# Third copies of VectorE's groups by an accumulating transfer onto a buffer filled with the constant, in a fused attention and GEGLU block

## The chip, the cores and the metric

The kernel runs on one core of one Trainium2 chip. The metric is the device time of one execution in microseconds; lower is better. Two runs of the kernel before gave 807.44 and 808.38 us, median 807.91.

## The reference

One transformer block over 2048 tokens of width 512, in bf16, with a modulation computed from a vector `c`:

```python
mod = (silu(c) @ w_mod).reshape(1, 6, 1, -1)          # sa, ca, ga, sb, cb, gb
h = layernorm(x) * (1 + ca) + sa
q, k, v = heads(h @ wqkv)                             # 32 heads of 16
p = softmax(q @ k.T * 16 ** -0.5)
x = x + ga * ((p @ v) @ wo)
h = layernorm(x) * (1 + cb) + sb
x = x + gb * ((gelu(h @ w_gate) * (h @ w_up)) @ w_down)   # 1792 wide
```

The heavy part off TensorE is the softmax: 32 heads x 2048 x 2048 exponentials.

## The kernel before

**A planner writes the order.** The program has no loops on the chip. Python code (class `_Recorder`, `rec` at L219) records each instruction with its reads and writes, works out the semaphore waits, and keeps a model of when each engine is free and when each transfer lands (`model`, L297; `ISSUE`, L52, and `MARGIN`, L55, are the allowances of each kind of transfer in ns). `stream` (L1441) chooses what comes next by that model: it asks with `probe` (L327) when a step's inputs will be there, and issues it if that is soon enough. What it writes is a fixed list for each engine, and on the chip each engine works through its list in order, waiting for semaphores. If something lands later than the model said, everything behind it on the waiting engine is late too.

**The units.** Attention is cut into 64 units: a set of query columns by a group of four heads that lie on the four row strips of TensorE. A unit is 512 (four of them, the first two interleaved), 256 (52) or 128 (8) query columns wide, and is worked in rounds: 16, 8 or 4 of them, by width. A round is one 128 x 512 bank of scores for each of the four heads, so 2048 banks in all. TensorE computes the scores into two sets of three PSUM banks (`ps_sc`), ScalarE takes the exponentials of a set in one instruction (1536 wide, or 1024 where one bank goes to VectorE) into a ring of 15 slots, `E`, and TensorE multiplies them with the values into `ps_pv` (`pv_mms`, L1792). The units' products are taken in order: a unit starts when the one before has ended.

**VectorE's groups.** ScalarE is relieved by VectorE, which takes whole rounds: four banks, one for each head, called a group (or quad). VectorE converts a bank of scores to 16-bit integers that, read as bf16, are a stepwise approximation of the exponential (`bits`, L1712, a multiply and add, 128 x 512, PSUM to SBUF, into one of the buffers `kq`). Then come three copies of the whole group, 128 x 2048, each with a constant added (`SHIFT` is 32, 64, 96), into the buffers `sq` (`shift_task`, L1804). The converted group and its three copies are multiplied with four scaled versions of the values (`vaug` and `vs`), and the sum evens out the steps. So a group costs VectorE four conversions and three copies, and TensorE four times the products of a round. There are nine `sq` slots by name; which of them may be used depends on the stage (`room`, L1511): the first four always after "modB" (the modulation of the second half, done early in the kernel), others while the memory they overlap is free. A copy's slot is given back when its product has been issued (L1609).

`plain[u]` counts the rounds of unit u whose products are still to be taken from `E`; a group taken from the unit lowers it by one.

**Everything else is side work** that fills TensorE's and VectorE's gaps: the projections, the output projection, the feed-forward network set by set, with its weights streamed through SyncE's queue (SP) in 256 KB pieces, and the denominators of the softmax, which travel through small transfers on the same queue (`unit_end`, L1826). `background` (L1348) issues such steps on SP and VectorE when the model says they are due. The Pool engine works only in the first microseconds and once more for a mask.

**The planner's rules.** Fourteen numbers say how eager the planner is: how much slack ScalarE must have before side work is issued, how many candidates for groups it looks ahead, and so on. They come from `TUNE` (L63), a row for each stage of 64 banks, 33 rows for 32 stages; `RULES` (L62) is a common row that three of the stages use unchanged.

**The fillers.** `short` (L1427) adds up the columns of matmul work (weighted by the share of the array that they use) that the planner has issued in the last 3413 ns, and compares the sum with `FILL`, 3700. Where there is less, and TensorE has time, the planner adds matmuls whose result nobody uses: the identity times a tile of `x` (L1661, L1757), or a product with zeros (L1762). A thin stretch also lets side work go ahead of its credit (L1743).

Of the kernel before, what the change touches and what calls it, by code (L numbers as in the profile page):

```python
# [6 lines left out]
ALU = mybir.AluOpType  # L7
# [4 lines left out]
U16 = mybir.dt.uint16  # L12
# [10 lines left out]
NKT = S_TOK // P  # L23
VW = DH + 1
EPS = 1e-5
FILL = 3700
HALF = 0
GELU_C = 0.044715
TANH_C0 = float(np.sqrt(2.0 / np.pi))
# [19 lines left out]
NS = 3  # L49
NSQ = 4  # L50
FLOW = sum(a + n <= 1536 for a, n in SETS)
ISSUE = {"dd": 462, "de": 630, "db": 610, "dc": 400, "st": 410, "sd": 530, "se": 530, "ws": 450, "wu": 420, "wg": 510, "wd": 480, "ou": 400, "qo": 620}  # L52
SAFE = 0
EARLY = (800, 1000, 800)
MARGIN = {"db": 1200, "dd": 1800, "de": 1500, "qo": 1500, "st": 2300, "dc": 1500, "ws": 1500, "sd": 2000, "se": 1700, "wd": 1700, "wu": 1500, "wg": 1500}  # L55
FIRST = (2, 1, 2, 3)
STOP = ('ln2',)
STOPAT = 0
# [1 line left out]
ROUND = 200  # L60
STEP = 64
RULES = (600, 3500, 6, 120, 700, 150, 2, 9, 96, 30, 2, 1536, 100, 150)  # L62
TUNE = (  # L63
# [33 lines left out]
)  # L97
END = (0, None)
WAIT = 250
SLIP = 100  # L100


# [26 lines left out]
class _Recorder:  # L129
# [292 lines left out]
    def dma(self, eng, out, in_, sem, noncontig=False, late=0):  # L422
# [8 lines left out]
        run = min(int(a.ap[-1][1]) * mybir.dt.size(a.dtype) for a in (out, in_))  # L431
        return self.rec(eng, fn, [in_], [out], dma=sem, cost=(n, run, MARGIN.get(sem[:2], 0) + late))

    def emit(self, final):
        for s in self.count:
            self.sem[s] = self.nc.alloc_semaphore(s)
        val = {}
        for s, ops in self.bystream.items():
            n = 0
            for op in ops:  # L440
                if s in COMPUTE:
                    n += 1 if op.inc else 0
                else:
                    n += 16
                val[(s, op.seq)] = n
        prog = {e: [] for e in ALLENG}
        for op in self.ops:
            waits = tuple((s, val[(s, n)]) for s, n in op.waits.items())

            def run(e, op=op, waits=waits):  # L450
                for s, v in waits:
                    e.wait_ge(self.sem[s], v)
                ins = op.fn(e)
                if op.stream not in COMPUTE:
                    ins.then_inc(self.sem[op.stream], 16)
                elif op.inc:
                    ins.then_inc(self.sem[op.stream], 1)
            prog[op.eng].append(run)
        for s in final:
            prog["sp"].append(lambda e, s=s: e.wait_ge(self.sem[s], 16 * self.count[s]))  # L460
        with self.nc.Block() as block:
            for eng, starter in (("sp", block.sync), ("act", block.scalar), ("pe", block.tensor),
                                 ("dve", block.vector), ("pool", block.gpsimd)):
                def body(e, fns=prog[eng]):
                    for f in fns:
                        f(e)
                starter(body)


class _Kernel(_Recorder):  # L470
# [12 lines left out]
    def alloc(self):  # L483
# [71 lines left out]
        self.pv = ps("ps_pv", [P, 512], FP32)  # L555
        self.mi = ps("ps_mi", [P, 512], FP32)
        self.scr2 = self.dram("scr_rec", [4, 2048], FP32)
        self.wdg = self.dram("wd_scaled", [F, D], BF16).rearrange("(f p) n -> p f n", p=P)


    def prologue(self):
# [15 lines left out]
        for k in range(3):  # L577
            self.dma(sp, wq4[:, :, k, P:D], wqv[:, :, k, P:D], "wr%d" % k)
        self.dma(sp, self.wmod[:, :, 1024:3072], wmv[:, :, 1024:3072], "wm2")

        half = self.half
        self.memset(dve, self.warm, 0.0)
# [729 lines left out]
    def step(self, eng, t):  # L1312

        hold = None
        for tk in sorted(self.tasks, key=self.urgency):
# [3 lines left out]
            if "last" in self.have and eng == "dve" and t is not None:  # L1319
# [3 lines left out]
                if self.urgency(tk) == -3:  # L1323
                    hold = x if hold is None else min(x, hold)
                    if x > max(t, self.free[eng] + WAIT):
                        continue
                elif x > t or (hold is not None and max(x, self.free[eng]) + self.probed > hold + SLIP):
                    continue
            elif t is not None and self.probe(f) > t:
                continue  # L1330
# [15 lines left out]
        return n  # L1346

    def background(self, t):  # L1348
        while self.step("sp", max(self.free["sp"], t) + 40):
            pass  # L1350
        while self.free["dve"] <= t + self.tune[13] and self.step("dve", max(self.free["dve"], t) + 40):
            pass

    def force(self):
        if not self.step("sp", None) and not self.step("dve", None):
            assert self.step("act", None)

    def plan(self, ends, nsplit, begin):
# [82 lines left out]
    def stream(self):  # L1441
# [59 lines left out]
        wait = []  # L1501
        self.quad_free = list(range(NK + 1))
        self.sq_free = list(range(len(self.sq)))
        self.holds = {}
        self.users = [0] * (NKT // 4)
        soon = units[:4] + [u for u in units[4:] if u[0] == (0,)]
# [88 lines left out]
        def pv_do(x):  # L1595
# [10 lines left out]
            else:  # L1606
                q["ready"].remove((i, src))
                q["n"] -= 1
                if i:  # L1609
                    self.sq_free.append(q["slots"].pop(i))  # L1610
                if q["n"] == 0:
                    wait.remove(q)
# [179 lines left out]
    def pv_mms(self, rnd, acc, src, i, first, last):  # L1792
# [3 lines left out]
        for kk in range(kpb):  # L1796
            kt = r * kpb + kk
            v = self.vs[:, i - 1, kt % 4, VW * 8 * (self.part_of(kt // 4, dc) - dc):] if i else self.vaug[:, kt, :]
            for j in range(4):
                h = 8 * dc + 2 * j + ee  # L1800
                self.mm(acc[32 * j:32 * j + VW, 0:W], v[:, VW * h:VW * h + VW], src[j][:, W * kk:W * kk + W],
                        start=first and kk == 0, stop=last and kk == kpb - 1, tp=(0, 32 * j))

    def shift_task(self, q, i):  # L1804

        def f():
            s = self.room(self.sq_free, q["rnd"][0])[0]
# [300 lines left out]
```

## Time and profile before

| | |
|---|---|
| median of two runs | 807.91 us |
| profiled execution, its own time | 808.1 us |
| span of its instructions | 806.4 us |
| conversions of scores on VectorE, in the three largest groups | 412 |
| transfers on SP's queue | 57.99 MB in 97216 packets |
| work of Pool | 4.9 us, 13 instructions |

Reading it: PE is TensorE's matmuls, PEld its weight loads, DVE is VectorE, ACT ScalarE, POOL GpSimd, SP SyncE. A row of instructions names line, engine and operation, the tile written and those read with their shapes, and the count; then busy microseconds in all and the mean nanoseconds of one; then the idle time of the engine ahead of them and what ended it. In a table by stretch each engine's busy time is given with the number of its instructions, then the clock that TensorE was granted (1.00 is full speed), the busy share of the 16 transfer engines, and GB/s. Most instructions go through a helper and carry its line, so a tile's name tells more than the line. The rows that matter are shown in the prediction.

### The profile page before, as it was taken

Reading aid. Unit: us, or ns where it says so; the run is one execution under the profiler, and the core shown is the slowest. Engines: PE = TensorE matmul, PEld = TensorE weight load, DVE = VectorE, ACT = ScalarE, POOL = GpSimd, SP = SyncE. Lnnn points to the kernel's source line nnn. Section 1 sums busy time; section 2 is a strip of 40 time slices with the busy share of each in tenths; the row PEclk is TensorE's granted clock in tenths of the full one; section 3 lists DMA queues with packets and bytes.
Section 4 is the critical chain, followed back from the end, with each engine's and each line's share of the span. In section 5 each row is a group of like instructions: output and inputs, shape, how many; then the busy total and the mean of one; then the engine's idle time right before and its main releaser. Section 6 shows DMA issues by size and latency. Waiting matters only on the chain.

```text
span 806.4 us, 37404 instructions
## 1 busy us (share of the span) xinstructions
PE 749.7 (93%) x17203; PEld 373.9 (46%) x17203; DVE 748.8 (93%) x1514; ACT 778.1 (96%) x729; POOL 4.9 (1%) x13
## 2 busy tenths in 40 slices
PE   8899999998999989998999999989998999999998
PEld 4334344343543455344544554445443554456566
DVE  7878999999999999989999999999999999999874
ACT  6999999999999999999999999999999999999982
POOL 2000000000000000000000000000000000000000
PEclk9999999999999999999999999999999999999999
DMA  9100012240550055003430542034233532200000
GB/s 302 59 12 12 25 36 63 62 118 13 151 148 21 18 144 154 25 15 114 122 93 16 140 121 55 22 107 125 71 78 91 160 100 79 81 11 12 24 6 15
DMA packets 97904, 60.92 MB, mean 76 GB/s; under 512 B 16913, under 2 KB 95378, under 8 KB 97746
## 3 DMA queue, kind: packets, MB, share of 16 engines
q1 hardware_dynamic: 97216, 57.99, 25.4%
q8 instruction: 135, 2.21, 1.2%
q10 hardware_dynamic: 530, 0.53, 0.2%
q14 instruction: 23, 0.19, 0.1%
HBM read 51.74 MB, written 4.18 MB: 69 GB/s over the span
## 4 chain that ended last, share of the span: by engine, by line
ACT 79%; PE 13%; DVE 6%; DMA 1%; issue 1%; SPq 0%; DVEq 0%
ACT E L377 76%; PE ps_sc L364 5%; PE ps_mi L364 5%; PE ps_pv L364 3%; ACT wreg L377 2%; DVE mreg L389 1%; DVE dreg L389 1%; DVE wreg L394 1%; DVE wreg L398 1%; DMA xs<-in_A_x_dram 0%; DMA mreg<-in_B_w_up_dram 0%; DVE wreg L381 0%; DVE kq L389 0%; DVE hreg L381 0%; DVE hreg L389 0%
## 5 line engine op out<-in xcount | busy, mean ns | idle before, releaser
L377 ACT ACTIVATE E<-ps_sc 128x1024 bf16<-128x1024 f32 (+2 forms) x683 | 752.0, 1309 | 14.2 <-PE ps_sc L364 13.7
L364 PE MATMUL ps_sc<-qo,kT 32*128 32x256 bf16 (+2 forms) x2048 | 195.8, 273 | 18.3 <-ACT E L377 14.9
L364 PE MATMUL ps_sc<-qT,kT 32*128 32x256 bf16 (+3 forms) x2048 | 196.3, 273 | 16.7 <-ACT E L377 13.2
L364 PE MATMUL ps_pv<-E,vaug 128*17 128x256 bf16 (+2 forms) x3188 | 154.4, 273 | 1.3 <-DVE vaug L398 0.5
L389 DVE TENSOR_SCALAR dreg<-ps_sc 128x512 uint16<-128x512 f32 x200 | 135.4, 683 | 5.4 <-PE ps_sc L364 4.3
L364 PE MATMUL ps_mi<-wreg,mreg 128*32 128x256 bf16 x2816 | 109.4, 275 | 6.1 <-DVE wreg L398 3.7
L364 PEld LDWEIGHTS ps_sc<-qo,kT 32*128 32x128 bf16 x2048 | 60.6, 92 | 108.7 <-ACT E L377 90.6
L364 PEld LDWEIGHTS ps_sc<-qT,kT 32*128 32x128 bf16 (+1 forms) x2048 | 60.9, 92 | 103.7 <-ACT E L377 79.6
L364 PEld LDWEIGHTS ps_pv<-E,vaug 128*17 128x17 bf16 x3188 | 61.3, 89 | 57.8 <-issue 36.5
L389 DVE TENSOR_SCALAR kq<-ps_sc 128x512 uint16<-128x512 f32 x112 | 75.7, 684 | 10.0 <-PE ps_sc L364 9.4
L364 PEld LDWEIGHTS ps_mi<-wreg,mreg 128*32 128x32 bf16 x2816 | 64.2, 96 | 39.2 <-issue 20.9
L389 DVE TENSOR_SCALAR mreg<-ps_sc 128x512 uint16<-128x512 f32 x100 | 67.1, 682 | 1.7 <-PE ps_sc L364 1.5
L364 PE MATMUL ps_pv<-mreg,vs 128*17 128x256 bf16 (+2 forms) x1504 | 67.0, 270 | 1.3 <-DVE mreg L389 1.2
L389 DVE TENSOR_SCALAR mreg<-dreg 128x2048 uint16<-128x2048 uint16 x90 | 60.1, 679 | 1.4 <-PE ps_pv L364 1.3
L364 PEld LDWEIGHTS ps_pv<-mreg,vs 128*17 128x17 bf16 x1504 | 33.0, 91 | 14.5 <-issue 5.7
L364 PE MATMUL ps_mi<-hreg,wreg 128*32 128x512 bf16 (+1 forms) x496 | 37.4, 377 | 0.4 <-DVE qT L389 0.3
L394 DVE SCALAR_TENSOR_TENSOR wreg<-wreg,ps_mi 128x512 bf16<-128x512 bf16 x49 | 33.2, 678 | 1.2 <-ACT wreg L377 0.9
L381 DVE TENSOR_TENSOR wreg<-wreg 128x1024 bf16<-128x1024 bf16 (+1 forms) x56 | 34.2, 611 | 0.1
L398 DVE CAST wreg<-ps_mi 128x512 bf16<-128x512 f32 x49 | 33.4, 682 | 0.7 <-PE ps_mi L364 0.3
L389 DVE TENSOR_SCALAR mreg<-mreg 128x2048 uint16<-128x2048 uint16 x49 | 33.0, 680 | 0.0
L377 ACT ACTIVATE wreg<-wreg 128x1024 bf16<-128x1024 bf16 (+1 forms) x28 | 29.7, 1062 | 0.0
L389 DVE TENSOR_SCALAR mreg<-kq 128x2048 uint16<-128x2048 uint16 x40 | 27.0, 682 | 0.3 <-PE ps_pv L364 0.2
(201 smaller groups left out, 782.9 us busy)
## 6 DMA issues: line engine op xcount, KB each, us to landing
mreg<-in_B_w_up_dram SPq DMA_DIRECT2D x46, 256.0 KB, 3.1
mreg<-in_B_w_gate_dram SPq DMA_DIRECT2D x42, 256.0 KB, 3.2
dreg<-wd_scaled SPq DMA_DIRECT2D x18, 256.0 KB, 3.8
rb<-scr_rec SPq DMA_DIRECT2D x116, 32.0 KB, 2.3
mreg<-wd_scaled SPq DMA_DIRECT2D x12, 256.0 KB, 4.5
ereg<-wd_scaled SPq DMA_DIRECT2D x12, 256.0 KB, 4.0
mreg<-in_w_mod_dram SPq DMA_DIRECT2D x1, 2048.0 KB, 12.8
out_dram<-xs SPq DMA_DIRECT2D x15, 128.0 KB, 1.7
```

What stands on the lines that cost most here:

```text
L364: return self.rec("pe", lambda e: e.matmul(out, lhsT, rhs, start=start, stop=stop, tile_position=tp), [lhsT, rhs], [out], cost=(n, int(rhs ...
L377: return self.rec("act", lambda e: e.activation(out, in_, func, scale=scale, **kw), rd, wr, cost=self.cost("act", out, [in_], "act"))
L381: return self.rec(eng, lambda e: e.tensor_tensor(out, a, b, op), [a, b], [out], cost=self.cost(eng, out, [a, b], "tt"))
L389: return self.rec(eng, lambda e: e.tensor_scalar(out, a, s1, s2, **kw), rd, [out], cost=self.cost(eng, out, [a], "ts") + 60 * (len(rd) - 1 ...
L394: return self.rec("dve", lambda e: e.scalar_tensor_tensor(out, a, s, b, op0=op0, op1=op1), rd, [out], cost=self.cost("dve", out, [a, b], " ...
L398: return self.rec(eng, lambda e: e.tensor_copy(out, in_), [in_], [out], cost=self.cost(eng, out, [in_], "ts"))
```

## The change

- For a group's third copy, where conditions hold, VectorE does nothing. A buffer of `sq` has been filled ahead with the constant 96 in every 16-bit element, by a transfer from a DRAM tensor of 128 x 2048 such elements (`prefill`, on SP, 512 KB); and a transfer issued from Pool adds the converted group onto it (`dma_add`, 512 KB, with `accum_op`). The product of that copy then waits for this transfer.
- The conditions: a filled buffer exists; and the unit still has at least `DISTANT` (13) times its width / 512 rounds in `plain`. Buffers are filled one at a time, after "modB" and before the last scores, while more than one slot is free and one of the first four is among them.
- The planner gets allowances for the two transfers: "px" (the fill) 500 ns of issue and 1000 ns of margin, "ax" (the addition) 1400 and 2500, and it counts the addition as three times its bytes (`ADDED`).
- In the prologue Pool writes the constant into one buffer, ahead of its other work, and SP stores it to DRAM behind the loads.
- `background` and `force` also step tasks on Pool.
- The rows of `TUNE` are replaced by 32 times `RULES`.
- `FILL` becomes 1 at the top of the file, and the same name is set again further down, where it is also the number of buffers filled ahead. `short` reads the same name, so its threshold is 1 column.

The diff, without the 33 rows that go:

```diff
-FILL = 3700
+FILL = 1
...
-ISSUE = {"dd": 462, "de": 630, "db": 610, "dc": 400, "st": 410, "sd": 530, "se": 530, "ws": 450, "wu": 420, "wg": 510, "wd": 480, "ou": 400, "qo": 620}
+ISSUE = {"dd": 462, "de": 630, "db": 610, "dc": 400, "st": 410, "sd": 530, "se": 530, "ws": 450, "wu": 420, "wg": 510, "wd": 480, "ou": 400, "qo": 620, "px": 500, "ax": 1400}
...
-MARGIN = {"db": 1200, "dd": 1800, "de": 1500, "qo": 1500, "st": 2300, "dc": 1500, "ws": 1500, "sd": 2000, "se": 1700, "wd": 1700, "wu": 1500, "wg": 1500}
+MARGIN = {"db": 1200, "dd": 1800, "de": 1500, "qo": 1500, "st": 2300, "dc": 1500, "ws": 1500, "sd": 2000, "se": 1700, "wd": 1700, "wu": 1500, "wg": 1500, "px": 1000, "ax": 2500}
...
-TUNE = (
...
-)
+TUNE = (RULES,) * 32
 END = (0, None)
 WAIT = 250
+DISTANT = 13
+ADDED = 3
+FILL = 1
+KEEP = 1
...
+    def dma_add(self, out, in_, sem):
+        n = mybir.dt.size(out.dtype)
+        for _, k in out.ap:
+            n *= int(k)
+        return self.rec("pool", lambda e: e.dma_start(out, in_, accum_op=ALU.add), [in_, out], [out], dma=sem, cost=(ADDED * n, 4096, MARGIN["ax"]))
...
+        self.scx = self.dram("shift_row", [P, 2048], U16)
...
+        self.memset(pool, self.sq[NSQ - 1].bitcast(U16), SHIFT[NS - 1])
+        self.dma(sp, self.scx, self.sq[NSQ - 1].bitcast(U16), "px_")
...
-                elif x > t or (hold is not None and max(x, self.free[eng]) + self.probed > hold + SLIP):
+                elif x > t or (hold is not None and max(x, self.free[eng]) + (self.probed if isinstance(self.probed, float) else 0) > hold + SLIP):
...
     def background(self, t):
+        if "modB" in self.have and "last" not in self.have and len(self.filled) < FILL and len(self.sq_free) > KEEP and min(self.sq_free) < NSQ:
+            self.prefill()
+        while self.step("pool", max(self.free["pool"], t) + 40):
+            pass
...
-        if not self.step("sp", None) and not self.step("dve", None):
+        if not self.step("sp", None) and not self.step("pool", None) and not self.step("dve", None):
...
+        self.filled = []
...
-                if i:
+                if i in q["slots"]:
                     self.sq_free.append(q["slots"].pop(i))
...
+    def prefill(self):
+        s = self.sq_free.pop(self.sq_free.index(next(x for x in self.sq_free if x < NSQ)))
+
+        def f():
+            self.dma("sp", self.sq[s].bitcast(U16), self.scx, "px%d" % s)
+        self.task([("sp", f)], ("px", s))
+        self.filled.append(s)
+
     def shift_task(self, q, i):
+
+        if i == NS - 1 and self.filled and self.plain[q["rnd"][0]] * 512 >= DISTANT * q["rnd"][0][3]:
+            s = self.filled.pop(0)
+
+            def g():
+                self.dma_add(self.sq[s].bitcast(U16), self.kq[q["k"]].bitcast(U16), "ax%d" % s)
+                if self.probing is None:
+                    q["slots"][i + 1] = s
+                    q["ready"].append((i + 1, [self.sq[s][:, 512 * x:512 * x + 512] for x in range(4)]))
+            self.task([("pool", g)], ("add", q["rnd"][0]), lambda: ("px", s) in self.have)
+            return
```

33 rows, old and new, of the table TUNE are left out of this document.

## The prediction

> **What bounds the kernel now.** I read the page first (busy shares, then the chain that ended last), then the busy time by stretch, then the groups of ScalarE and VectorE by form.
>
> ```profile
> span 806.4 us, 37404 instructions
> ...
> PE 749.7 (93%) x17203; PEld 373.9 (46%) x17203; DVE 748.8 (93%) x1514; ACT 778.1 (96%) x729; POOL 4.9 (1%) x13
> ...
> ACT 79%; PE 13%; DVE 6%; DMA 1%; issue 1%; SPq 0%; DVEq 0%
> ```
>
> ```profile
> 20.00:780.00 760.00, 710.48 (x16676) 346.88 (x16673) 721.91 (x1428) 757.43 (x698) 0.56 (x1) 1.00 0.26 72
> 340.00:360.00 20.00, 18.86 (x389) 8.10 (x386) 18.01 (x35) 19.39 (x19) 0.00 (x0) 0.91 0.06 16
> ```
>
> The columns of the second fence are the stretch, then busy us of PE, weight loads, DVE, ACT and POOL, granted clock, DMA share and GB/s. Between 20 and 780 us ScalarE idles 2.6 of 760 us and VectorE 38: the exponentials on ScalarE set the end, and VectorE, which takes what rounds it can off ScalarE, is nearly as full. So freed VectorE time is worth something only through more rounds moved over to it. POOL does nothing, and the DMA share is 0.26: both have room.
>
> ```profile
> L377 ACT ACTIVATE E<-ps_sc 128x1536 bf16<-128x1536 f32 x282 | 416.2, 1562 | 2.7 <-PE ps_sc L364 2.4
> L377 ACT ACTIVATE E<-ps_sc 128x1024 bf16<-128x1024 f32 x393 | 398.0, 1143 | 1.1 <-PE ps_sc L364 0.9
> ```
>
> ```profile
> L389 DVE TENSOR_SCALAR dreg<-ps_sc 128x512 uint16<-128x512 f32 x200 | 135.4, 683 | 5.4 <-PE ps_sc L364 4.3
> L389 DVE TENSOR_SCALAR kq<-ps_sc 128x512 uint16<-128x512 f32 x112 | 75.7, 684 | 10.0 <-PE ps_sc L364 9.4
> L389 DVE TENSOR_SCALAR mreg<-ps_sc 128x512 uint16<-128x512 f32 x100 | 67.1, 682 | 1.7 <-PE ps_sc L364 1.5
> L389 DVE TENSOR_SCALAR mreg<-dreg 128x2048 uint16<-128x2048 uint16 x90 | 60.1, 679 | 1.4 <-PE ps_pv L364 1.3
> ```
>
> ```profile
> 219.29 1.89 DVE L389 TENSOR_SCALAR mreg<-dreg 128x2048 uint16<-128x2048 uint16 x3
> 221.20 0.69 DVE L398 CAST wreg<-ps_mi 128x512 bf16<-128x512 f32 x1
> ```
>
> The first three VectorE rows are conversions, 412 of them, so 103 groups of four. A copy lasts 679 ns, but three in a row take 1.89 us and the next instruction starts 1.91 us after the first: instructions overlap, and a copy, or a conversion, costs 0.6 to 0.64 us of the queue. I take 0.60. A group costs VectorE 4 conversions and 3 copies, 4.2 us. It saves ScalarE four times the difference between an activation of 1536 and one of 1024, 4 x (1562 - 1143) ns = 1.68 us.
>
> **The change, part by part.**
>
> (1) Copies off VectorE. A 256-wide unit has 8 rounds. Its first group leaves a count of 7, and 7 x 512 is over 13 x 256; its second leaves 6, which is too few. So at most one group a unit is served: the 52 units of that width, less those at whose turn no filled buffer waits or a round has been consumed, and less those before "modB", plus two or three 512-wide ones. I take 45 copies, bounds 25 and 52. VectorE saves 45 x 0.60 = 27 us. Both engines are full and must end together, so with x more groups ScalarE shortens by 1.68x and VectorE's load by 27 - 4.2x; equal at x = 27 / 5.88 = 4.6 groups, and the kernel by 1.68 x 4.6 = 7.7 us. With 25 copies it is 4.3, with 52 it is 8.9. A filled buffer takes one of four copy buffers while it waits; cover is the three others and those that some stages add. A group's own buffer is held until its addition's matmuls, some 9 us instead of 2; groups come 680 us / 100 = 6.8 us apart, so two are held at a time, of four. If that cover is gone, groups are refused and the term shrinks: the last rival.
>
> (2) The fillers. The name FILL now stands twice and is 1, also for the rule that adds matmuls when TensorE's work of the last 3.4 us is under 3700 columns. They vanish. The stretches below lie on the grid of 3413 ns on which the clock changed.
>
> ```profile
> 86.23:89.64 3.41, 2.75 (x53) 1.36 (x50) 3.38 (x9) 3.41 (x4) 0.00 (x0) 1.00 0.00 0
> 192.04:195.45 3.41, 2.36 (x44) 0.73 (x36) 2.11 (x10) 3.41 (x4) 0.00 (x0) 1.00 0.05 7
> 618.66:622.07 3.41, 2.53 (x46) 1.00 (x46) 2.39 (x11) 3.41 (x3) 0.00 (x0) 1.00 0.28 68
> 352.45:355.86 3.41, 2.27 (x48) 0.84 (x46) 3.35 (x6) 3.41 (x4) 0.00 (x0) 1.00 0.00 0
> 355.86:359.27 3.41, 3.41 (x56) 1.44 (x59) 3.15 (x7) 2.82 (x3) 0.00 (x0) 0.50 0.04 7
> ```
>
> The same stretches, fillers alone (the columns are now PE, weight loads, DVE, POOL, clock, DMA):
>
> ```profile
> 192.04:195.45 3.41, 1.01 (x12) 0.35 (x12) 0.00 (x0) 0.00 (x0) 1.00 0.05 7
> 618.66:622.07 3.41, 0.93 (x12) 0.44 (x12) 0.00 (x0) 0.00 (x0) 1.00 0.28 68
> ```
>
> After the emptiest stretch (2.27 us busy) the next ran at half clock; TensorE lost 1.7 us of 3.41, and ScalarE idled 3.41 - 2.82 = 0.59 us. Without their 1.01 and 0.93 us of fillers two other stretches would be at 1.35 and 1.60 us, below it. With similar places early in the kernel I take seven such stretches: 7 x 0.59 = 4 us. Bounds: 0, if new work lies there, and 7 x 1.7 = 12 us. The Trainium skill ("TensorE: Matmul & The Clock Gate", "Why this matters for your kernels") says that one idle window of about 3 us takes the clock down; by that rule gaps as short as these cost nothing and this term would be 0. The trace differs: 2.27 busy us of 3.41 were followed by half clock, and I go by the row.
>
> (3) Fills and additions. A fill moves 512 KB by SP, an addition 512 KB by POOL.
>
> ```profile
> mreg<-in_w_mod_dram SPq DMA_DIRECT2D x1, 2048.0 KB, 12.8
> ...
> mreg<-in_w_mod_dram ACTq DMA_DIRECT2D x1, 512.0 KB, 4.8
> ```
>
> A fill should land in about 4.8 us; it is issued as soon as the one before is used, so about a unit's time (680 us over 50 units, 13.6 us) ahead of its own use: nothing there. On SP it passes the denominators' small transfers and weight loads, each fill 0.5 us of issue and 1.6 us of transfer (512 KB at the 320 GB/s that the planner assumes). SP has the time: it waits for others much of the span.
>
> ```profile
> SPq L427 <- PE ps_mi L364: 91.4, 39, 9.8
> SPq L427 <- DVE osb L398: 90.2, 16, 18.1
> ```
>
> Nothing else stands on POOL behind an addition. It reads both operands and writes one: no row shows one. Bounds: 4.8 us as one load of the size, 12.8 us as the 2 MB load. The planner sets aside 0.9 + 1.5 MB / 320 GB/s = 4.9 + 1.0 + 2.5 = 9.3 us, above the middle of these. TensorE runs in order, so an addition later than that holds TensorE, and ScalarE behind it once its two sets of three banks are drained. I take 3 us in all for lateness and for denominators behind large transfers. Bounds: 0, and 45 x (12.8 - 9.3) = 157 us of TensorE wait, of which a third reaches ScalarE (0.59 of 1.7 us in the rows under (2)), 54 us. I stay near the low end: the nearest row, the load of the same size, leaves 4.5 of the 9.3 us unused.
>
> (4) The rules by stage become one set. No arithmetic is removed; the order of side work, groups and copies changes everywhere. Bounds from the first stretches: an order as good as now gives 0. One as loose all along as 340 to 360 us, with ScalarE idle 0.61 us and VectorE 2.0, loses 0.61 + 2.0 x 1.68 / 5.88 = 1.2 us in each of 34 stretches, 41 us, less what is lost now (2.6 + 38 x 0.29 = 13 us), so 28 us more. I take a quarter, 7 us: three of the present stages already hold exactly the one set, so it is no bad set, but the others were set apart from it.
>
> (5) The constant. POOL's first instruction becomes a fill of 2048 elements, ahead of the two that VectorE's reduction waits for.
>
> ```profile
> 4.05 1.26 POOL L405 MEMSET rb<- 128x1024 f32 x1
> ```
>
> ```profile
> 2.41 0.15 DVE L413 TENSOR_REDUCE rm<-den 128x1 f32<-128x4 f32 x1
> 2.48 0.07 DVE L405 MEMSET modA<- 128x4 f32 x2
> 2.59 0.15 DVE L389 TENSOR_SCALAR rm<-rm 128x1 f32<-128x1 f32 x1
> 3.64 0.69 DVE L417 BATCH_NORM_STATS2 st<-xs 128x6 f32<-128x512 bf16 x1 [0.90 <-DMA xs<-in_A_x_dram]
> 4.37 0.18 DVE L420 BATCH_NORM_AGGREGATE mv<-st 128x2 f32<-128x6 f32 x1
> 4.47 0.15 DVE L394 SCALAR_TENSOR_TENSOR sc_bf<-tcol,ps_sc 128x4 bf16<-128x4 f32 x1
> 4.91 0.69 DVE L417 BATCH_NORM_STATS2 st<-xs 128x6 f32<-128x512 bf16 x1 [0.29 <-DMA xs<-in_A_x_dram]
> ```
>
> At 1.26 us per 1024 elements it lasts 2.5 us. The reduction then starts at 4.9, the first statistics at 2.74 + 2.5 = 5.24, the second 0.98 later at 6.2 instead of 4.91: 1.3 us on the path to the first exponential. If it takes 1.26 us, 0.1. I take 1.3. The store of the constant is queued on SP behind the loads and has the gap up to the first fill as cover.
>
> **Sum.** The profiled execution took 808.1 us (span 806.4 and 1.7 around it), 0.2 over the median of 807.9. 808.1 - 7.7 + 4 + 3 + 7 + 1.3 = 815.7; I say 815.5 against the median.
>
> **Rivals.**
>
> The gain wins. The order keeps its tightness, (2) and (4) cost 2 us between them, and additions are in time: 807.9 - 7.7 + 2 + 1.3 = 803.5. For it speaks that DMA and POOL are empty and that 9.3 us is a generous allowance; against it that four terms must be small together. Under 791.7 it cannot come by these terms.
>
> The addition lands late. It is issued just when VectorE starts the two other copies of its group. Any delay beyond 9.3 us is a TensorE wait at once, since a copy is used when it is due. With 1.3 us each (two copies of 0.6 and the pool's own start), 45 x 1.3 = 58 us of TensorE wait and a third on ScalarE, 19 us: 815.5 + 19 = 834.5. It outweighs (1) from 45 x d / 3 = 7.7, so from d = 0.5 us. Against it stand the 4.5 us that a plain load of the size leaves unused. The Trainium skill ("SBUF — State Buffer", "Who interferes with whom") says that VectorE in its two-port mode shuts GpSimd out, and that a transfer stalled by VectorE is one whose descriptors GpSimd writes; by that rule this rival is the likely one. No run here shows a transfer issued from POOL.
>
> The single rule set is loose: (4) costs 20 instead of 7: 828.5. VectorE idle well above 38 us would show it.
>
> The change does not do what it says: buffers are so scarce that under ten fills find a place. (1) shrinks to 1.7 us, (3) to 1: 815.5 + 6 - 2 = 819.5.
>
> **Numbers.** The forecast (808 to 823) 0.45, the gain wins 0.22, late additions 0.15, loose rules 0.10, few fills 0.08. Between 800 and 838 lie all but a sixth: the far ends of late additions and of a gain with 52 copies are left out; the forecast's own range is 808 to 823. About 2% is what a measurement of this kernel can tell from no change: below 791.7, 0.03, of the gain's 0.22; above 824.1, 0.23, four fifths of late and loose together and 0.03 of the forecast; within, 0.74.
>
> **What would show it.** Step 1: copies fewer by about 45, conversions up by 4 x 4.6 = 18, and as many POOL transfers. Step 2: stretches at half clock, about eight against one. Step 3: an issue-to-landing time of additions over 9 us, and TensorE waiting for them. Step 4: VectorE and ScalarE idle between 20 and 780 us. Step 5: the first exponential 1.3 us later. I am wrong if the additions hold TensorE by microseconds each, or if idle time does not grow at all.

## The result and the profile after

The changed kernel takes 864.42 us in both runs compared, beside 807.91 before: a ratio of 1.0694, 95% interval 1.0664 to 1.0724. The forecast was 815.5, range 800 to 838. The profiled execution has a span of 862.7 us against 806.4. Of one experiment below (e8_not_booked) the profiled execution was disturbed, 865.9 us beside 851.3, 852.6 and 856.3 in the runs compared, so its rows are used only for the kind of its waits.

The page of the kernel after: span, busy shares, granted clock by slice, SP's and POOL's transfers (packets, MB, share of 16 engines' time), and the chain that ended last.

```profile
span 862.7 us, 36933 instructions
...
PE 778.7 (90%) x16932; PEld 383.0 (44%) x16937; DVE 720.2 (83%) x1447; ACT 787.7 (91%) x730; POOL 49.1 (6%) x60
...
PEclk9699999989999989999999998999999997899799
...
q1 hardware_dynamic: 104128, 83.16, 32.7%
q0 software_dynamic: 6624, 24.12, 15.5%
...
ACT 59%; PE 33%; DVE 6%; issue 1%; POOL 0%; DVEq 0%; POOLq 0%
```

SP's queue before, for comparison:

```profile
q1 hardware_dynamic: 97216, 57.99, 25.4%
```

TensorE's part of the chain went from 13 to 33%: ScalarE now often waits for scores. 6912 more packets on SP are 48 transfers of 144 packets (47 fills and the store of the constant); POOL's 6624 are 46 additions, so one fill was never used. Over the whole span ScalarE's busy time rose by only 9.6 us; its idle time rose from 28.3 to 75.0, by 46.7.

By stretch, the kernel after (the columns are those of the prediction):

```profile
20.00:780.00 760.00, 691.39 (x14993) 324.56 (x14993) 655.14 (x1275) 727.60 (x664) 43.02 (x47) 0.95 0.53 136
780.00:862.70 82.70, 71.04 (x1729) 50.32 (x1733) 50.47 (x120) 47.73 (x49) 0.00 (x0) 0.93 0.05 13
```

Between 20 and 780 us ScalarE idles 32.4 us instead of 2.6, VectorE 104.9 instead of 38.1, and TensorE 68.6 instead of 49.5. No engine is full any more. The transfers' share doubled, 0.26 to 0.53. The granted clock fell from 1.00 to 0.95.

VectorE's groups by form, then ScalarE's and TensorE's waits, in the kernel after:

```profile
L359 DVE TENSOR_SCALAR dreg<-ps_sc 128x512 uint16<-128x512 f32 x196 | 133.1, 687 | 26.1 <-PE ps_sc L334 24.6
L359 DVE TENSOR_SCALAR kq<-ps_sc 128x512 uint16<-128x512 f32 x108 | 73.7, 687 | 15.5 <-PE ps_sc L334 15.3
L359 DVE TENSOR_SCALAR mreg<-ps_sc 128x512 uint16<-128x512 f32 x96 | 65.2, 687 | 11.6 <-PE ps_sc L334 11.2
L359 DVE TENSOR_SCALAR mreg<-dreg 128x2048 uint16<-128x2048 uint16 x59 | 40.0, 687 | 2.9 <-PE ps_pv L334 2.9
```

```profile
ACT E L347 <- PE ps_sc L334: 60.5, 60, 12.8
...
PE ps_sc L334 <- ACT E L347: 47.2, 128, 0.9
```

The same wait of ScalarE before:

```profile
ACT E L377 <- PE ps_sc L364: 13.7, 16, 2.1
```

Conversions in the three largest groups are 400, twelve fewer than before (412): VectorE was freed of 46 copies and took three groups fewer. The idle time ahead of these conversions rose from 17.1 to 53.2 us, and what ended it were scores from TensorE. ScalarE waited for scores 60.5 us instead of 13.7. TensorE's matmuls waited in turn for ScalarE to empty a bank, never longer than 0.9 us, and TensorE waited for no addition and no fill: the only transfer in its list is a first load of 0.6 us. So the obvious suspect, a late addition, isn't there. The landings agree (KB each, median us from issue to landing):

```profile
mreg<-shift_row SPq DMA_DIRECT2D x35, 512.0 KB, 4.6
mreg<-in_B_w_up_dram SPq DMA_DIRECT2D x46, 256.0 KB, 4.2
mreg<-in_B_w_gate_dram SPq DMA_DIRECT2D x42, 256.0 KB, 4.6
mreg<-dreg POOLq DMA_DIRECT2D x20, 512.0 KB, 5.7
```

The additions land after 5.7 us in the largest group (the medians of all groups lie between 5.5 and 7.4), inside the 9.3 that the planner allows, the fills after 4.6. The list of instructions that each engine works through is simply slacker, and the trace alone doesn't say why. The experiments were chosen for that.

### The profile page after: what moved, and what is told of

Read it like the earlier page. It is cut to its first block, busy times and chain, and to the rows that moved or that the text cites. A ratio compares the mean times of both kernels' runs of the same rounds, so it can differ in the third digit from the quotient of the medians.

```text
span 862.7 us, 36933 instructions
## 1 busy us (share of the span) xinstructions
PE 778.7 (90%) x16932; PEld 383.0 (44%) x16937; DVE 720.2 (83%) x1447; ACT 787.7 (91%) x730; POOL 49.1 (6%) x60
## 3 DMA queue, kind: packets, MB, share of 16 engines
q1 hardware_dynamic: 104128, 83.16, 32.7%
q0 software_dynamic: 6624, 24.12, 15.5%
## 4 chain that ended last, share of the span: by engine, by line
ACT 59%; PE 33%; DVE 6%; issue 1%; POOL 0%; DVEq 0%; POOLq 0%
ACT E L347 57%; PE ps_mi L334 13%; PE ps_sc L334 11%; PE ps_pv L334 9%; ACT wreg L347 2%; DVE mreg L359 1%; DVE wreg L364 1%; DVE osb L368 1%; DVE dreg L359 1%; DVE xs L351 0%; PE ps_mi L338 0%; DVE st L387 0%; DVE hreg L359 0%; DVE wreg L368 0%; POOL sq L375 0%
## 5 line engine op out<-in xcount | busy, mean ns | idle before, releaser
L347 ACT ACTIVATE E<-ps_sc 128x1024 bf16<-128x1024 f32 (+2 forms) x684 | 760.7, 1279 | 61.1 <-PE ps_sc L334 60.5
L334 PE MATMUL ps_sc<-qT,kT 32*128 32x256 bf16 (+3 forms) x2048 | 212.3, 281 | 30.2 <-ACT E L347 24.5
L334 PE MATMUL ps_sc<-qo,kT 32*128 32x256 bf16 (+2 forms) x2048 | 213.1, 284 | 24.9 <-ACT E L347 22.7
L334 PE MATMUL ps_pv<-E,vaug 128*17 128x256 bf16 (+2 forms) x3208 | 161.1, 282 | 7.9 <-DVE osb L368 3.5
L334 PEld LDWEIGHTS ps_sc<-qo,kT 32*128 32x128 bf16 x2048 | 66.3, 94 | 119.4 <-ACT E L347 89.3
L359 DVE TENSOR_SCALAR kq<-ps_sc 128x512 uint16<-128x512 f32 x108 | 73.7, 687 | 15.5 <-PE ps_sc L334 15.3
L334 PE MATMUL ps_pv<-mreg,vs 128*17 128x256 bf16 (+2 forms) x1304 | 61.1, 281 | 0.8 <-DVE mreg L359 0.8
L359 DVE TENSOR_SCALAR mreg<-dreg 128x2048 uint16<-128x2048 uint16 x59 | 40.0, 687 | 2.9 <-PE ps_pv L334 2.9
L351 DVE TENSOR_TENSOR xs<-xs,ps_mi 128x512 bf16<-128x512 bf16 x30 | 20.5, 684 | 25.5 <-PE ps_mi L334 25.3
L408 POOL DMA_DIRECT2D mreg<-dreg x20 | 18.6, 928 | 294.7 <-DVE dreg L359 283.0
L368 DVE COPY osb<-ps_pv 128x256 f32<-128x256 f32 (+2 forms) x63 | 26.2, 416 | 6.4 <-PE ps_pv L334 6.0
```

Of the source, the lines that this page charges most:

```text
L334: return self.rec("pe", lambda e: e.matmul(out, lhsT, rhs, start=start, stop=stop, tile_position=tp), [lhsT, rhs], [out], cost=(n, int(rhs ...
L347: return self.rec("act", lambda e: e.activation(out, in_, func, scale=scale, **kw), rd, wr, cost=self.cost("act", out, [in_], "act"))
L351: return self.rec(eng, lambda e: e.tensor_tensor(out, a, b, op), [a, b], [out], cost=self.cost(eng, out, [a, b], "tt"))
L359: return self.rec(eng, lambda e: e.tensor_scalar(out, a, s1, s2, **kw), rd, [out], cost=self.cost(eng, out, [a], "ts") + 60 * (len(rd) - 1 ...
L368: return self.rec(eng, lambda e: e.tensor_copy(out, in_), [in_], [out], cost=self.cost(eng, out, [in_], "ts"))
L408: return self.rec("pool", lambda e: e.dma_start(out, in_, accum_op=ALU.add), [in_, out], [out], dma=sem, cost=(ADDED * n, 4096, MARGIN["ax"]))
```

## The experiments

Each time is set against runs of the kernel before on the same chip. A difference between two experiments is that of their ratios, times 808 us; it is uncertain by some 3 us.

**The other parts of the change, without additions.** Three runs: the fillers' threshold alone, the rules alone, and the changed kernel without fills and additions.

```diff
 e1_no_fillers (before)
-FILL = 3700
+FILL = 1
 e2_one_rule_set (before)
-TUNE = ( ... 33 rows ... )
+TUNE = (RULES,) * 32
 e3_no_additions (after)
-... and len(self.filled) < FILL and ...
+... and len(self.filled) < 0 and ...
```

> The kernel before with FILL at 1 alone. Theory A (the loss of 56 us lies in the order that the planner writes around the additions): a few stretches at half clock, each worth 0.6 us, 812 us. Theory C (the fillers' absence and the half clock are the main loss: 26 stretches of 3.4 us at half clock after, against 1): over 825 us.

> The kernel before with the one rule set for all stages alone. Theory A: 815 us, as in the prediction's step 4. A rival in which the stage rules carry the loss: over 830 us.

> The changed kernel without fills and additions: one rule set, no fillers, the constant still made in the prologue; every third copy is VectorE's again. Theory A: 820 us (807.9 + 4 + 7 + 1.3). Theory C and the rival of the rules: 850 us or more, since both of their causes stay.

Measured: 824.61 us (1.0215, 1.0181 to 1.0248), 822.07 (1.0164, 1.0139 to 1.0190), 820.81 (1.0158, 1.0131 to 1.0184). Each costs 13 to 17 us, and both together no more than either alone. The first is just under the 825 us of its Theory C. So everything but the additions costs 1.58%, 12.8 us, and the fills and additions bring the other 43 of the 56. The threshold and the rules don't add up: they may share something else than fillers or looseness, which the next two runs looked for.

e13_thin_fillers keeps the order of before and makes the fillers one column wide, so they are issued and do almost no work. e14_one_number_changed keeps the fillers and raises one number of the rules, the third, by one in every stage.

```diff
 e13_thin_fillers (before, in the matmul helper)
+        o, r = out, rhs
+        if (lhsT is a filler's):
+            o, r = out[:, 0:1], rhs[:, 0:1]
 e14_one_number_changed (before)
-        self.tune = TUNE[min(i, len(TUNE) - 1)]
+        x = list(TUNE[min(i, len(TUNE) - 1)])
+        x[2] += 1
+        self.tune = tuple(x)
```

> The kernel before with its order to the last instruction; each filler matmul is 1 column wide in place of 512 or 256. If the fillers' absence costs by the half clock alone: 820 to 825 us, as without fillers. If most of that run's 16 us came from the order that the threshold changes: 809 to 813 us, the prediction's step 2.

> The kernel before with the third of the planner's fourteen numbers, the length of VectorE's backlog at which no new group is begun, 1 higher in each stage, and nothing else. If the rules are fitted to this one order, so that any other plan is looser: 815 to 820 us. If they are merely good: 806 to 810 us.

Measured: 816.81 us (1.0098, 1.0077 to 1.0118), between the two ranges named, and 819.41 (1.0130, 1.0103 to 1.0156). The work of the fillers is thus worth 7.9 us with the order unchanged, and what changed with it is the clock. Stretches of e13 on the grid of its clock, each thin one ahead of the half clock that follows:

```profile
196.80:200.21 3.41, 1.99 (x49) 0.94 (x46) 2.60 (x7) 3.41 (x4) 0.00 (x0) 1.00 0.13 28
200.21:207.04 6.83, 6.83 (x98) 2.80 (x102) 5.57 (x11) 5.36 (x6) 0.00 (x0) 0.50 0.07 17
367.46:370.88 3.42, 2.50 (x46) 1.09 (x46) 2.84 (x11) 3.42 (x4) 0.00 (x0) 1.00 0.17 26
370.88:374.29 3.41, 3.41 (x58) 1.36 (x56) 2.33 (x6) 2.81 (x4) 0.00 (x0) 0.50 0.14 22
```

With 1.99 and 2.50 busy us of 3.41, the next stretches ran at half clock, and ScalarE idled 1.47 us in the first (of two lengths) and 0.60 in the second. Busy time alone doesn't decide it, though: in the kernel before, the stretches with 2.36 and 2.53 busy us, 1.01 and 0.93 of them fillers, were followed by full clock. The profile's clock of e13 is

```profile
core 0: 814.7 us, clock 0.981
```

so (1 - 0.981) x 2 x 814.7 = 31 us, nine stretches, were at half clock, against (1 - 0.998) x 2 x 806.4 = 3 us, one, before: eight stretches for 7.9 us, 1.0 us each on average. And one number raised by one costs 10.5 us with the fillers in place. I read it so that the 33 rows are fitted to one particular order; leaving that order cost 10 to 13 us in three runs that left it in different ways (e2, e3, e14).

**Fills and additions on the two backgrounds.** e5_additions_alone is the kernel before with the fills and additions (and the constant in the prologue), and nothing else; e4_fillers_back is the changed kernel with the threshold back at 3700.

```diff
 e4_fillers_back (after)
-FILL = 1
+FILL = 3700
...
-FILL = 1
+AHEAD = 1
...
-        if ... len(self.filled) < FILL and ...
+        if ... len(self.filled) < AHEAD and ...
 e5_additions_alone: the same, and the 33 rows of TUNE put back
```

> The changed kernel with the fillers' threshold at 3700 again under a name of its own; fills, additions and the one rule set stay. Theory A: 855 to 865 us, since the additions stay. Theory C: 26 stretches less at half clock, 1.7 us of TensorE each, 820 us.

> The kernel before with fills and additions alone: its rules by stage and its fillers stay. Theory A (the order around the additions): 840 to 850 us. If the loss needs all three parts together: under 820 us.

Measured: 864.96 us (1.0712, 1.0667 to 1.0756) and 845.18 (1.0448, 1.0430 to 1.0465). With the tuned rows and the fillers, fills and additions still cost 4.48%, 36 us. With the fillers back in the changed kernel the granted clock rises and the time doesn't fall:

```profile
core 0: 869.0 us, clock 0.974
```

Against 0.948 that is about half of the half-clock time gone, for nothing; but the threshold changes the order too. e5 bounds the clock's share better:

```profile
core 0: 842.3 us, clock 0.990
```

That is (1 - 0.990) x 2 x 842.3 = 17 us, five stretches at half clock, four more than before. At 1.0 us each, an estimate from e13, they are 4 of its 36 us. So fills and additions cost most of their price with the clock nearly full.

**What freed time of VectorE is worth.** In e6_copies_left_out the third copy of the groups that the additions would serve isn't made at all: its product reads the converted group itself. This leaves out the addition of 96 for 51 groups. e12_left_out_one_rule_set does the same with the one rule set.

```diff
 e6_copies_left_out (before, in shift_task)
+        if i == NS - 1 and "modB" in self.have and "last" not in self.have and self.plain[q["rnd"][0]] * 512 >= 13 * q["rnd"][0][3]:
+            kq = self.kq[q["k"]]
+            q["ready"].append((i + 1, [kq[:, 512 * x:512 * x + 512] for x in range(4)]))
+            return
...
```

> The kernel before, with the third copy left out for groups that meet the same condition: VectorE does nothing there, no transfer is issued, and the product reads the converted group itself, so one of four terms of those groups is wrong. It measures what freed VectorE time is worth at most. The prediction's step 1: 47 x 0.60 us freed, 800 us. Rival: the planner gives the time to no new group, 807 to 810 us.

> The kernel before with the one rule set, and with the third copies of the groups that meet the condition left out (the product reads the converted group, so these terms are wrong). Against 822 us of the one rule set alone it prices freed VectorE time away from the tuned rules. The prediction's step 1: 814 us. Rival: 822 us, freed time finds no use there either.

Measured: 809.15 us (1.0011, 0.9997 to 1.0025) and 818.04 (1.0135, 1.0114 to 1.0156), the latter 2 to 4 us under e2 (1.0164; 822.07), with intervals that overlap, and midway between the two times named for it. So 51 copies taken away at no price at all bring nothing in the kernel before. As e6 also leaves the order to which the rows are fitted, a gain could hide behind that loss; e12 against e2, both with the one rule set, speaks against more than some 4 us. Rows fitted anew to the freed time were not tried. e6 by stretch, and ScalarE's wait for scores:

```profile
20.00:780.00 760.00, 712.00 (x16730) 349.51 (x16729) 707.41 (x1398) 753.33 (x697) 0.56 (x1) 1.00 0.26 72
```

```profile
ACT E L377 <- PE ps_sc L364: 18.8, 18, 2.6
```

VectorE's idle time grew by 14.5 us (721.9 to 707.4 busy): about half of the 51 x 0.60 = 31 us freed. The rest paid for three more groups, and ScalarE's busy time fell by 4.1 us in this stretch; but ScalarE's idle time grew by the same 4.1, and its wait for scores from 13.7 to 18.8 us over the whole span.

**The transfers, or the plan for them.** Four runs cross two things: whether the planner books the fills and additions on its one queue of transfers, and whether the bytes are moved. In e7_small_transfers the order of the changed kernel is kept, and each fill and addition moves 32 of 2048 columns (most of the third copy's values are missing). In e8_not_booked the planner gives each its own landing time, without pushing back the other transfers. e9_not_booked_small is e8 with 32 columns; e15_small_additions is e8 with whole fills and additions of 32 columns.

```diff
 e8_not_booked (after, where the planner's model books a transfer)
+            if op.stream[2:4] in ("px", "ax"):
+                op.t1 = t + 900 + size / 320 + 1000 + margin
+                return
 e7_small_transfers (after), e9_not_booked_small (e8)
-... e.dma_start(out, in_, accum_op=ALU.add) ...
+... e.dma_start(out[:, 0:32], in_[:, 0:32], accum_op=ALU.add) ...
-            self.dma("sp", self.sq[s].bitcast(U16), self.scx, "px%d" % s)
+            o, i = self.sq[s].bitcast(U16), self.scx
+            self.rec("sp", lambda e: e.dma_start(o[:, 0:32], i[:, 0:32]), ..., cost=(128 * 4096, 4096, MARGIN["px"]))
 e15_small_additions (e8): only the additions cut
```

> The changed kernel with its order to the last instruction, but each fill and each addition moves 32 of 2048 columns, so the third copies of 47 groups are wrong. Theory A: the order costs the time whatever the transfers take, 855 to 864 us. Theory B (the additions' transfers land late or crowd the other transfers out): under 835 us.

> The changed kernel, but the planner does not book fills and additions on its one serial transfer queue: each still gets its own time to land, and other transfers are planned as if these were not there. Theory A: the order gets tight again, 820 to 830 us. Theory B: more additions and weight loads meet unplanned, late landings hold TensorE and VectorE, 864 us or more.

> The order of the run without booking, to the last instruction, with fills and additions that move 32 of 2048 columns (third copies of the groups concerned are wrong). If that run's 854 us came from transfers that crowd denominators and weights out: 820 to 830 us. If its order itself is slow: 845 us or more.

> The order without booking again (854 us with whole transfers, 820.7 with small ones), with whole fills and additions of 32 of 2048 columns (these third copies are wrong). If the additions crowd the others out: 821 to 828 us. If the fills do: 845 to 854 us. Both alike: 835 to 840 us.

Measured, as ratios (before = 1):

| | bytes moved | hardly any bytes |
|---|---|---|
| booked | 1.0694 (after) | 1.0585 (1.0541 to 1.0630), 858.2 us (e7) |
| not booked | 1.0551 (1.0516 to 1.0585), 851.3 to 856.3 us (e8) | 1.0164 (1.0142 to 1.0186), 820.7 us (e9) |
| not booked, fills whole | | 1.0191 (1.0145 to 1.0238), 824.84 us (e15) |

Read down the last column: booking alone, with hardly a byte moved, costs 1.0585 - 1.0164 = 4.2%, 34 us. Read along the second row: moving the bytes, unbooked, costs 3.9%, 31 us, of which the fills account for 0.3% (within the intervals, nothing) and the additions, beside whole fills, for the rest. So e8's 854 us, which lies in neither of its two ranges, is a tighter order that pays for its bytes. Read along the first row: booked, the bytes cost 1.1%, 9 us. Most of the price is paid once, either in the plan or on the chip. And e9, with its additions nearly free and unbooked, is no better than e3 without them (1.0164, 1.0158).

The booked order is slack in itself. Whether that comes of the one queue or of counting an addition as three times its bytes was not tested. e7 has ScalarE's long wait with almost no bytes:

```profile
ACT E L347 <- PE ps_sc L334: 56.7, 57, 12.8
```

```profile
20.00:780.00 760.00, 693.60 (x15167) 326.75 (x15169) 658.56 (x1283) 731.22 (x668) 42.73 (x47) 0.95 0.28 73
```

against e9, the same edits unbooked:

```profile
ACT E L350 <- PE ps_sc L337: 25.2, 31, 3.9
```

```profile
20.00:780.00 760.00, 702.89 (x16230) 344.04 (x16229) 690.39 (x1350) 749.04 (x687) 46.85 (x50) 0.98 0.28 74
```

The transfers' share is the same 0.28; ScalarE works 17.8 us and VectorE 31.8 us more in e9. How far each had come is seen in the exponentials still to do from 770 us on, in e7 and then in e9:

```profile
L347 ACT ACTIVATE E<-ps_sc x44: 383/1047/1469, 770.3 to 851.4; 128x1536 bf16<-128x1536 f32 x21, 128x1024 bf16<-128x1024 f32 x14, 128x512 bf16<-128x512 f32 x7, 128x256 bf16<-128x256 f32 x2
```

```profile
L350 ACT ACTIVATE E<-ps_sc x26: 384/1028/1498, 769.7 to 810.9; 128x1536 bf16<-128x1536 f32 x9, 128x1024 bf16<-128x1024 f32 x8, 128x512 bf16<-128x512 f32 x7, 128x256 bf16<-128x256 f32 x2
```

On the chip, unbooked, the crowding falls on others. Waits for transfers in e8 (engine, tile and line that waits, releaser: us in all, times, longest):

```profile
DVE onorm L354 <- DMA rb<-scr_rec: 11.2, 4, 3.4
...
PE ps_mi L337 <- DMA mreg<-in_B_w_gate_dram: 6.2, 2, 5.3
...
DVE rden L374 <- DMA den<-osb: 5.8, 2, 3.1
...
PE ps_mi L337 <- DMA mreg<-in_B_w_up_dram: 2.2, 2, 1.6
```

These are the denominators' small transfers and the weights, and neither e9 nor the kernel after has such a wait. e15 has three short waits of this kind, 2.7 us on weights and 1.7 us on a denominator.

**POOL as a compute engine.** e10_fills_by_pool fills the buffers by POOL's memset instead of a transfer; e11_copies_on_pool gives the third copies to POOL as ordinary instructions, in the kernel before. e11 also raises one number of the rules by 150.

```diff
 e10_fills_by_pool (after)
-            self.dma("sp", self.sq[s].bitcast(U16), self.scx, "px%d" % s)
-        self.task([("sp", f)], ("px", s))
+            self.memset("pool", self.sq[s].bitcast(U16), SHIFT[NS - 1])
+        self.task([("pool", f)], ("px", s))
 e11_copies_on_pool (before, in shift_task; eng is "pool" for the copies concerned)
-            self.ts("dve", self.sq[s].bitcast(U16), self.kq[q["k"]].bitcast(U16), float(SHIFT[i]), None, ALU.add)
+            self.ts(eng, self.sq[s].bitcast(U16), self.kq[q["k"]].bitcast(U16), float(SHIFT[i]), None, ALU.add)
...
```

> The changed kernel with the fills written by the Pool engine instead of a transfer from DRAM, the constant's prologue gone; additions stay and stay booked. If the additions' booking makes the order slack (they are booked at three times their bytes, the fills at one): 850 us or more. If the fills' 25 MB are the burden: 835 us or less.

> The kernel before, with the same third copies computed by the Pool engine itself, no fill and no transfer; the sixth of the planner's fourteen numbers is 150 higher in each stage. If only the way through the transfers was wrong: 803 to 810 us. If Pool and VectorE get in each other's way: over 820 us, with longer copies on VectorE.

Measured: 899.6 us (1.1142, 1.1102 to 1.1182) and 1100.5 (1.3623, 1.3585 to 1.3660), both far worse. In e11 the copies of POOL and the largest group of VectorE's own:

```profile
L390 POOL TENSOR_SCALAR mreg<-dreg 128x2048 uint16<-128x2048 uint16 x18 | 97.4, 5410 | 237.2 <-DVE dreg L390 122.2 <-PE ps_sc L365 58.7 <-PE ps_pv L365 56.3
```

```profile
L390 DVE TENSOR_SCALAR mreg<-dreg 128x2048 uint16<-128x2048 uint16 x74 | 116.0, 1570 | 1.0 <-PE ps_pv L365 0.9
```

A copy lasts 5.41 us on POOL, and the largest group of VectorE's copies grows from 679 to 1570 ns on average. In e10 POOL's largest group of fills, and the same form of VectorE's copy:

```profile
L375 POOL MEMSET mreg<- 128x2048 uint16 x34 | 66.9, 1968 | 279.0 <-PE ps_pv L334 246.6 <-PE ps_mi L334 32.4
```

```profile
L359 DVE TENSOR_SCALAR mreg<-dreg 128x2048 uint16<-128x2048 uint16 x63 | 47.5, 762 | 0.3 <-PE ps_pv L334 0.2
```

In this form a copy lasts 75 ns more than in the changed kernel, in others more still (881 against 686 for `mreg<-kq`, 1019 against 685 for `hreg<-kq`). Over all forms VectorE's 253 copies take 208.3 us, against 175.4 us for 257 in the changed kernel. The order differs too, and the two weren't separated, so what made e10 35 us slower than the changed kernel stays open. For the same reason its 899.6 us doesn't tell whether the additions' booking or the fills' was the burden.

## Why the prediction was wrong

**Step (3), fills and additions, is the one that failed.** It put them at 3 us, on the reading that POOL and the transfers at a share of 0.26 "have room", and looked for their price mostly in an addition that comes late. The additions were in time, and still the fills and additions cost 43 us over e3. The step looked at what the new transfers wait for, and too little at what they push aside. One such cost it named and put within the 3 us, denominators behind large transfers: unbooked, the bytes cost 31 us, and the denominators' transfers and the weights are then waited for (e8 against e9). The other it left out: it worked out the planner's allowance for one addition, 9.3 us, but not what 46 of them do to the plan of everything else. The planner holds one queue for all transfers and books each addition on it as three times its bytes, and the order written so costs 34 us with hardly a byte moved (e7 against e9). The kernel after pays the second and 9 us of bytes. That the booking pushes back side work, leaves TensorE's gaps unfilled and so starves both other engines is how I read e7's rows; shown is only that the booking makes the difference. Part of the 34 us may be the clock's: by their mean clocks (0.946 and 0.985) e7 has 27 stretches at half clock and e9 seven, which at e13's price would be 20 us. e4, where half of the stretches went and the time stayed, and e5, where they are 4 us of 36 at that price, speak against so large a part; for e7 itself it isn't settled.

From run to run the way to the measured time is: 808 + 12.8 (all but the additions, e3) + 0.5 (additions placed, neither booked nor moved, e9) + 34 (booked, e7) + 9 (bytes moved) = 864.

**Step (1), copies off VectorE.** The count was right: 45 forecast, 46 made. The worth, 7.7 us, was 0 in e6, and 2 to 4, not clear of noise, in the one-rule order (e12). The failed assumption is that VectorE and ScalarE "must end together": half the freed time stayed idle, and what the three further groups saved, ScalarE lost waiting for scores. Nor did the freed time come back as groups in the kernel after, which has three fewer, not 4.6 more.

**Step (2), the fillers: right in kind, too small.** Eight stretches at half clock came where seven were forecast, at 1.0 us each instead of 0.59: 7.9 us for 4 (e13; the 1.0 is an average). Taking the threshold out as the change does costs 9.5 more (e1 at 17.4), since the planner also chooses differently. On the one rule set it costs nothing more (e3 against e2). In the kernel after, the clock of 0.948 means (1 - 0.948) x 2 x 862.7 = 90 us, 26 stretches, not eight; but with half of them gone e4 is no faster. The rule of the Trainium skill ("TensorE: Matmul & The Clock Gate", "Why this matters for your kernels"), an idle window of about 3 us, would have made this term 0. The rows of e13 are against it here as the row of before was: 2.0 and 2.5 busy us in a stretch were followed by half clock.

**Step (4), one rule set.** 7 forecast, 13 measured (e2), inside the bounds of 0 and 28. The reason given for a small value ("no bad set") was beside the point: one number raised by one costs 10.5 us (e14). What is lost is, as I read it, the fit of the rows to one order.

**Step (5), the constant in the prologue.** POOL's memset took 1.8 us of the 2.5 forecast, and the first exponential starts at 13.10 instead of 12.84 us: 0.26 us later, not 1.3. The memset in the kernel after:

```profile
L375 POOL MEMSET sq<- 128x2048 uint16 x1 | 1.8, 1804 | 0.3 <-POOLq L2096 0.3
```

**The rivals.** The late addition had the nearest time but the wrong mechanism: landings of 5.7 us in the largest group, no wait of TensorE for one. So of the two signs named for being wrong neither came, as idle time did grow; the forecast failed in a way that they don't cover. The sign named for the loose rule set did come, VectorE idle well above 38 us (104.9), and it would have misled: the rule set alone costs 13 us and leaves VectorE idle 54.7 us in the same stretch (e2). For the late addition, the rule of the Trainium skill ("SBUF — State Buffer", "Who interferes with whom") says that VectorE's two-port mode and POOL lock each other out, and that transfers whose descriptors GpSimd writes stall by it. For the transfers no run here shows it: 46 of them went beside VectorE's copies, which stay at 687 ns (679 before), and landed in time. For POOL's own instructions the trace agrees on VectorE's side, 1570 ns a copy (e11); POOL's 5.41 us has no undisturbed value beside it here.

The chance given to a time above 824.1 us was 0.23, and none of its cases reached 864. The upper bound of 54 us for step (3) would have, but by additions that hold TensorE, which didn't happen; that it is near the 43 us measured is chance.

No version here beats the kernel before. With freed VectorE time worth 0 to 4 us, a cheaper way of making the third copies can bring no more than that with the rules as they stand; with rules fitted anew to it, that is not known.

## What to carry to other kernels

Before paying for a way to free an engine, leave the work out (as e6 does) and see what the freed time is worth: here 0 to 4 us. Of an added transfer, ask what it pushes aside, in the plan as well as on the chip, and not only whether it is in time itself. A tuned schedule can be fitted to one order, so compare both arms with the same tuning, and allow for a change of order that costs something in itself (here 10 to 13 us in three runs) before the idea is judged.

## What the hardware showed

An accumulating transfer of 512 KB within SBUF took more time of the 16 transfer engines than a plain load of 512 KB from DRAM: POOL's queue took 15.5% of 862.7 us for 24.12 MB, 134 us or 5.5 us per MB, while the 25.2 MB that SP's queue moved more took 32.7% of 862.7 less 25.4% of 806.4 us, 77 us or 3.1 us per MB. The second figure is a difference of two kernels. The addition nevertheless lands soon, after 5.7 us in the largest group. And eight stretches at half clock cost about 1.0 us each on average (e13).
